# A new hand-out of one order for 1,418 steps on five engines

## The chip, the cores and the metric

The kernel runs on one core of a Trainium2 chip. The metric is device time in microseconds (us). TensorE (PE) multiplies matrices, VectorE (DVE), ScalarE (ACT) and GpSimd (POOL) do elementwise work, SyncE (SP) issues all transfers on one queue. Each engine works through its own list of instructions in order, and waits where an operand or a buffer isn't ready.

## The reference

A linear attention with a decaying state, and behind it a token-mixing and channel-mixing network. B, H, S, D = 4, 8, 768, 48, so the model width is 384; everything is float32.

```python
for t in range(S):                       # per batch and head
    cur = np.einsum('bhd,bhe->bhde', u[None] * kt, vt)
    y[:, :, t] = np.einsum('bhd,bhde->bhe', rt, state + cur)
    state = wt[:, :, :, None] * state + np.einsum('bhd,bhe->bhde', kt, vt)
...
h = xt @ U @ V                           # x: attention's result, mixed over time, rank 32
u = x + h.transpose(0, 2, 1)
ch = np.maximum(u @ w_ch1, 0.0) @ w_ch2  # 384 -> 1536 -> 384
return u + ch
```

## The kernel before, in words

**Staging.** The sequences are cut into chunks of 128 tokens: 24 chunks g, six for each batch. The network works on seven blocks of tokens, 384, 384, 512, 512, 512, 384 and 384 wide. Blocks 0 and 1 hold the first batch, blocks 5 and 6 the last, and blocks 2 to 4 the two between; a block can start as soon as its chunks and the mixing of their batches are done. So attention of later chunks and the network of earlier blocks run side by side, and blocks 5 and 6 wait for the last batch.

**Steps.** The kernel first makes a list of 1,418 named steps (`step`), each a small function with an engine, the steps it comes after, and the buffers it takes and uses. Nothing is issued then. Names carry the chunk, the weight part or the block with its part:

- Transfers (SP): LW, LRK, LKR, LV load decay, r and k, and v of a chunk (L359 to L371); LRAW a part of the weights (L284); LCK loads a part again for the check at the end; OUT sends a result (L919).
- Weights, which are split in a high and a low float32 part: E (L309), C2 (L302), C3 (L315), ADD (L322), HI (L332, L334), SUB (L339).
- Attention of chunk g: the scans F (L390) and Q (L405), each two instructions, with T (L397, L399) and R (L437, L438) between; RP (L413) and KS (L418, L420, a pair) scale r and k; PR (L418, L420) and MD (L496), or RK (L448), RU (L451) and RED (L455), make the diagonal; SEL and SEL2 (L469 on ScalarE, L475 on GpSimd) place it; KT, KN or KD (L522, L531, L679) turn k; AM (L544) gives the scores, CP (L551) masks them; DS (L561), ZA (L593) and ZM (L593 to L602) carry the state; YA and YZ (L622 to L649) give y; XE (L666) copies it out.
- Turning x: XT and XN (L735, L739) or, from chunk 12 on, XD2 and XD1 on VectorE (L716, L714), four steps of four transposes each.
- Mixing for a batch: GA (L761), G4 (L767), SELM (L772), GS (L776), GSL (L781).
- A block's network: HP (L815), UADD (L820), UH (L825, L827), UL (L831); then, for 12 parts f, UP (L864, nine matmuls), HH (L869 on ScalarE, L871 on VectorE) and HL (L875); then, for 3 column parts of 4 steps each, DN (L898, nine matmuls), and O (L916).
- CK and CM (L1083, L1089) look over the weights that LCK has loaded; GUARD (L429) does that for the decay.

**What sets the order.** A string ORDER, L62 to L103, three characters for each step. The first two are the step's number in base 64. The third says how: if it is odd the step runs on its second engine (`alt`, such as VectorE in place of ScalarE for an HH, or GpSimd in place of VectorE for an RP), and half of it is the number of warm-up matmuls on a blank tile that are issued ahead of the step (`lead`). `plan` (L131) reads the string, hands out the buffer slots in that order, first freed first, and returns the list; L1138 to L1140 then issue the steps. An engine's own list is thus the order of its steps in the string, and a transfer's place on SP's queue and its buffer come from it too. Slots: 20 big ones, two each for decay, v, F, turned k and state, one for Q, three PSUM tiles for the matmuls with `f`, `hp`, `ga`, `gb` and the turned tiles in common.

```python
i, how = DIGITS.index(ORDER[n]) * 64 + DIGITS.index(ORDER[n + 1]), DIGITS.index(ORDER[n + 2])
...
if how % 2:
    s.eng = s.alt
s.lead = how // 2
for buf in s.take:
    buf.slot = free[buf.pool].pop(0)
```

Of the kernel before, what the change touches and what calls it, by code (L numbers as in the profile page):

```python
# [59 lines left out]

DIGITS = "0123456789ABCDEFGHIJKLMNOPQRSTUVWXYZabcdefghijklmnopqrstuvwxyz+-"
ORDER = (  # L62
    "2x02y03002z03203M00J03713603303P00K03N03R03n03m03503412-03800L03V03C03903E03W13A13B10M03X03S03113v04B03U03F0"
# [4 lines left out]
    "0z04U10+01D07g14q00Z05504W00o07u00a04t04X01E04s05D00b00s07x00c05C17a03L00p01F04v04w07h04u15E01G03k05008300e0"
    "7c00q08014x04803l04905F07i18K05G00d17z05H04Y04y00r15I00-04Z01H10u04z08U05K05J01I00g05L07b07j15M07m05N00v07k0"
    "7W00f01007+00h00t07n05O07y15P07qC1101205Q07-18o08N00i07l05R00j00w05U05Y05V07r05S01d08A05Z00k07s05W08w05T17o0"  # L70
    "8L01W05a08108801J08901P05X11e07t05b11315o48V15l01f07p18415+08W15p01Q01K01g01L00x01X05m05q08501M00y08611N05-1"
    "5c01h06005d07w05f05n01O11Y01r06108711R08C01Z06201S08B01i08P05g01T01a08F02A09e08X06305e08G06S05h08Q05i08x08D0"
    "1k01b06T01j18T01U08Y11V15x01s02C01m08H08R01c08O05j05r08S08y11n08n05y02B05z05k02308z01t08c02D01u01l01o02E08m0"
    "5s07Y18Z15t06708M01y01v08p08d06801p01q08r08v08E11w02O02F06405u06901x11+02502402H08+11-02605v01z08h06U02008i0"
    "6502G12V09n08u16A02106B06605w08s02709M02I02202808a09h08t08j06C06W02P02J08b06D02Q08q12K02L02916E08-18e02M06X0"
    "2R08f09202X09002N02S09C09309102j08g12l06G06V12c02Y06a02T06H09402W02Z09E09709802k02a08k09F09N18l02U19906I02b1"
    "6b06Y09g09i16Z16F06c08I09A02m09H02e06d16J08J02f02q02d06K06h09I09L09D02g09B06i19j02s09506j09O16t06M02n06n09o0"
    "2o02h12t06u16o06v07602r09K16p02i19f02u09P09J07902p02v06N06O0B709Q19R0B80771Bh07A0BH09G12w09U07B09k09616w06x0"
    "BA06y0780BG0BY06P09S09T09p09q06z09m09V0BF0BX0BC09l16Q09r06k0BD07306+06L09W0Ba06l16m06R0BE19u0BI17409Z09s0BJ0"
    "9a09t19X0750C109v0C206q06-0BB06e0B909Y1C406f0Bc0BK09b0BN0700710BR06r09w0CB06g0C90Bd09x0Be1Bg0BO09c0C516s0CA0"  # L80
    "D70BL0BP0BQ09y0BM1CT0Bb17C0Bi07D0Bf0CC07209z09d07E09+0C60DZ07F0Cd0C709-0Bj0Cz0Bn0BS0BT0BV0A00Ce1Bk0BU1Br0A10"
    "CW0A20A30Bo0Da0Bl0CV07I0Bm0D80BZ07J0CU07K0Bp0CH0CI0CD07G0A40A50C81D60CE0A60Bs0A707L0A90D90AA07O0Bq0DA0Cf0DQ0"
    "C+0AB0AD0CJ0A80AE0Cb0HW07P07Q07R0AF0CF0CG17M0D00Bt07H0AC0Bu0G60CK0AG0Cg0CX1BW0Cj0Db0CL0H00CY0Bw0Bx07S07N0AQ0"
    "AT0HX0CZ0Ca1GW0Cc0Ck0C30D20Ac0AR0DP0AS0AW0AU0GX0CM07T0DB1Cn0Cl0Ch0CN0By0D50CQ0AV0DS0GN0Ad0DC1AX0Dc0F+0Bv1Bz0"
    "CR0Ai0Ae0D10CO0AY0Aj0CP1D30GY0Ci1AZ0D41DD0AN0CS0Aa0Ak0Cm0AO0HY0DE0DU0AP0AH0Co0Al0Cp0Fy0DH0DX0Cs0Ct0DV0G70DF0"
    "Ab0DT1Cq0Am0AI0F-0DW1AK0DI0Cr1DY0An0Cu0AJ0Ao0C-0B+0DM0DG0GM0DN0Dd0AL0Cv0G50Df0DJ0Af0Ap0AM0G10DR0De0Ku0DK0GZ0"
    "Ar0Dg0DO0G20Aq0Ga0Cw0GP0DL1Ag0As0Ah0Gs0Dh0Di0At0Cx0Dj0Dk0Dl0Au0B-0Dm0G80Cy0C00Dn0Ax0Ay0G90H10Av0Fz0Az0G31G40"
    "GR0Lh0GQ1A+0G00A-0Do0Dp0Dq0GG0Dr0Ds0H20GS0Gb1B10GC0Dt0Du0Dv0Dy0H30B20GV0GA1E00GD0Gt0B30GU0Dz0E10Dw0Gv0D+0Gx0"
    "Dx0B40IS0E20E31Lq0GE0HM0GO0Gc0D-0EG0EH0LV0GB1E40Gw0HP0G+1Aw0E50G-0HN0B50IT1E60Ls0IU0Eb0EI0EJ0GF0Li0EV0HU0HQ1"
    "EK0Gd0Ec0Lj0H40HZ0EL0EM0EW0Ed0GI0GH0EN0GK0Kv0GT1Gg0Ew0LS0Ge0HO0I00EO0Kw0GJ1EX0B60Gh0Ex0Hc0ES0Gy0LT0Gz1Gf0ET1"  # L90
    "H51EA0LU0B00E70II0EU0Gi0HR0LX0LW0GL0Lr0Gl0IV0Gm0E80HA0EB0HS0ED0E90Ha1HV0EC0EE0H60Gn0EF0LJ0Hb0Hd0IL0I10EY0Ee0"
    "EP0L70HB0EQ0I21IR0Hs0EZ0Gu0Gj0I30Ht0ER0Gk1Ea0Ef0Eg0Hv0E+0H70E-0F20HT0Eh0Ek0H80Hx0Ey0H+0He0HF0HG0H90LL0Hy0Hg0"
    "F00HC0F30El0Ei0L80Em0En0IJ0I60LK0HH0Eq0I70F40Er0Hu0Hz1HD0Es0K+0F51L40I41Hf0Et0Go0HI0F10IN0Ez1HE1LY0IW1Ln0Hh0"
    "HJ0Gp0FR0IM0L90I50Eo0I80FS0I90FL0Eu0HK0K-0FI0Ej0Hl0Ev0FM1IO0Hm0Hi0HL0IA0FN0Hw1FJ0FT0Hj0Hk1Lt0Gq0Ep0F90IB0LD0"
    "Hn0F60IX0F70IC0Kr0FA1IP1La0IF0IG0IQ0FK0Ho0F80ID0Lv0Lp0IE1L00Hp0LZ0IY0FF0L60FG0FO0FB0FX0Gr0Hq0IZ0FP0IH0IK0Hr0"
    "Ia0FQ0Ib0FY0LA0Ih0Lu0Lo0FH0FC0FZ0Ic0Id0Ie0FD0FE0Fa0If0Ig0Fg0Kt0Ii0Fb0Ij0LF0Ik0Fh0Il0Im0Fc0In0Ir0Io0Is0Jp0Ip0"
    "Iv0Jq0Jt0Iw0M00Ju0Ks0L50FU0Fd0Fe0It0FV1FW0Lw0Fi0Ff0H-0Iq0Fj0Fm0Ix0Fn0Iu1Iy0Jr1Fo0Fk0Fp0Fs0Ft0Fq0JC0JR0M10Fu0"
    "JS1JT0Fv0JD0Lz0Fw0J00JE0Js0JF0Jv1Lx0LB0J10Jx0Le0LC0J20M20Iz0JG0Jy0Ly0J30J40LM0Lg0L-0I+1I-0LE0Lf0J50JU0J90JH0"
    "Lb0JO0JA0L10JV1JB0J60JP0JW0JI0JQ0JL0J70JM0J80JN0JX0JY0JJ0L+0Jz0JK0Fr0JZ0Ja0Jd0Fl0Jb0Je0Kx0Jf0Jg0Jj0Lk0Jk0Ld0"
    "LP0Jw0J+0Jh0LG0Ll0KQ0KR0Lm0KS0Ji0LR0Fx0KB0Jl0L20KC0KT0KU0L30LQ0Jm0KD0KV0KK0KL0LO0Jc0KM0J-0Jn0KH0Lc0LH0KI1KE0"  # L100
    "KJ0K01KF0KG0K80K50K10K20K60K91M30Kz0LN0K70KN0K30K40KO1M50LI0KA0M40Ky0KZ0KW0KX1Ka0KP0Kb0M60KY0M70M80Kc0Kf0Kg0"
# [1123 lines left out]
```

## Time and profile before

| what | value |
|---|---|
| time, median of 3 runs | 435.9 us (435.53 to 438.2) |
| the profiled execution: time, span | 435.73 us, 433.9 us |
| mean granted TensorE clock | 0.969 |
| instructions | 10499 |
| PE, DVE, ACT, POOL busy | 417.4, 344.5, 188.7, 137.7 us |
| moved by transfers | 57.29 MB |

The span goes from the first instruction of the program to the end of the last; the time also holds what lies around it. Busy time counts what overlaps once. Ends of matmuls are modelled, so a short wait between matmuls can be hidden in a busy PE.

### The profile page before, as it was taken

The page shows a single profiled execution, that of the slowest core. Times are in us where ns is not written, and L with a number is a line of the kernel's source. Part 1 is how long each engine was busy: PE and PEld are TensorE (multiplying, and loading weights), DVE is VectorE, ACT ScalarE, POOL GpSimd, SP SyncE. Part 2 cuts the span into 40 slices and gives each one's busy share as a digit, 9 for nine tenths or more (in the row PEclk, how much of TensorE's full clock was granted, in tenths as well). Part 3 has the DMA queues.
Part 4 walks back from the last instruction along what each step waited for, and adds up shares of the span by engine and source line. Part 5 has one row for each costly group of instructions (what it writes and reads, how often), then busy time and mean ns, then how long its engine had stood idle before and what let it go on. Part 6 is the DMA issues. An engine that isn't in the chain of part 4 may idle for free.

```text
span 433.9 us, 10499 instructions
## 1 busy us (share of the span) xinstructions
PE 417.4 (96%) x4150; PEld 361.9 (83%) x4150; DVE 344.5 (79%) x791; ACT 188.7 (43%) x536; POOL 137.7 (32%) x182
## 2 busy tenths in 40 slices
...
GB/s 281 330 283 263 296 168 213 112 191 160 255 147 190 99 269 126 44 49 135 7 155 127 162 95 48 79 184 141 52 22 39 0 133 98 73 105 66 2 39 42
DMA packets 23913, 57.29 MB, mean 132 GB/s; under 512 B 2864, under 2 KB 7856, under 8 KB 23856
## 3 DMA queue, kind: packets, MB, share of 16 engines
...
q8 instruction: 34, 0.56, 0.5%
...
HBM read 51.81 MB, written 4.72 MB: 130 GB/s over the span
## 4 chain that ended last, share of the span: by engine, by line
PE 73%; DVE 18%; ACT 3%; DMA 2%; issue 2%; POOL 0%; DVEq 0%
PE f L898 29%; PE f L864 25%; PE aps L544 4%; DVE kn L679 3%; DVE xn L716 3%; PE y L622 2%; DVE hid L875 2%; DVE xn L714 2%; PE dS L561 2%; PE y L632 2%; DMA v<-in_vS 2%; DVE A L551 1%; PE trd L496 1%; DVE F L390 1%; PE trk L522 1%
## 5 line engine op out<-in xcount | busy, mean ns | idle before, releaser
L864 PE MATMUL f<-u,w1h 128*128 128x384 f32 (+1 forms) x504 | 147.7, 364 | 1.8 <-DVE hid L875 1.1
L898 PE MATMUL f<-hid,w2h 128*128 128x384 f32 (+1 forms) x504 | 148.1, 364 | 0.0
L864 PEld LDWEIGHTS f<-u,w1h 128*128 128x128 f32 x504 | 92.9, 188 | 14.5 <-DVE hid L875 2.9
L898 PEld LDWEIGHTS f<-hid,w2h 128*128 128x128 f32 x504 | 92.9, 188 | 10.1 <-issue 0.7
L869 ACT ACTIVATE hid<-f 128x384 fp32r<-128x384 f32 (+1 forms) x67 | 35.9, 541 | 138.3 <-PE f L864 124.7
L864 PE MATMUL f<-u,w1l 128*128 128x384 f32 (+1 forms) x252 | 90.8, 360 | 0.0
L898 PE MATMUL f<-hid,w2l 128*128 128x384 f32 (+1 forms) x252 | 90.7, 360 | 0.0
L875 DVE SCALAR_TENSOR_TENSOR hid<-f,hid 128x384 fp32r<-128x384 f32 (+1 forms) x84 | 49.8, 608 | 22.0 <-ACT hid L869 21.0
L898 PEld LDWEIGHTS f<-hid,w2l 128*128 128x128 f32 x252 | 47.4, 188 | 4.7
L864 PEld LDWEIGHTS f<-u,w1l 128*128 128x128 f32 x252 | 47.4, 188 | 4.1
L679 DVE STREAM_TRANSPOSE kn<-rk 32x128 f32<-32x128 f32 x160 | 48.3, 302 | 2.4
L469 ACT ACTIVATE A<-ident,dv 128x128 f32<-128x128 f32 x136 | 43.0, 394 | 4.3 <-PE f L898 4.2
L916 DVE TENSOR_TENSOR xT<-f,xT 128x384 f32<-128x384 f32 (+1 forms) x21 | 12.8, 610 | 35.5 <-PE f L898 35.4
L322 POOL TENSOR_TENSOR cva_w<-cva_w,raw_w 128x384 int32<-128x384 int32 x24 | 26.1, 1098 | 45.4 <-ACT raw_w L309 18.6
L831 POOL TENSOR_TENSOR u<-xT,u 128x512 fp32r<-128x512 f32 (+1 forms) x11 | 12.8, 1169 | 85.4 <-ACT u L825 64.3
L413 POOL TENSOR_TENSOR rk<-rk,Q 128x512 f32<-128x512 f32 x18 | 21.6, 1201 | 52.3 <-DVE Q L405 34.9
L405 DVE TENSOR_TENSOR_SCAN Q<-w,starts,qd 128x258 f32<-128x258 f32 x48 | 33.2, 732 | 0.3
L551 DVE COPY_PREDICATED A<-maskf,aps 128x1024 f32<-128x1024 uint32 x24 | 31.5, 1311 | 0.3 <-PE aps L544 0.2
L390 DVE TENSOR_TENSOR_SCAN F<-w,qd 128x259 f32<-128x259 f32 x48 | 30.4, 673 | 1.2 <-DMA w<-in_wT 0.8
L716 DVE STREAM_TRANSPOSE xn<-xT 32x192 f32<-32x192 f32 x80 | 29.6, 370 | 1.1
L544 PE MATMUL aps<-rk 48*64 48x128 f32 (+1 forms) x768 | 24.2, 270 | 0.9 <-POOL rk L413 0.9
L544 PEld LDWEIGHTS aps<-rk 48*64 48x64 f32 x768 | 20.7, 147 | 5.1 <-issue 2.8
...
## 6 DMA issues: line engine op xcount, KB each, us to landing
...
```

What stands on the lines that cost most here:

```text
L322: lambda: nc.gpsimd.tensor_tensor(out=d["to"].bitcast(I32), in0=d["a"].bitcast(I32), in1=d["e"], op=ALU.add),
L390: nc.vector.tensor_tensor_scan(out=back(F), data0=back(st["w"]), data1=back(qd, OVER * h), initial=1.0, op0=ALU.mult, op1=ALU.add)
L405: nc.vector.tensor_tensor_scan(out=st["Q"][:, a:e], data0=st["w"][:, a:e], data1=qd[:, a - OVER * h : e - OVER * h], initial=starts[:, h : ...
L469: nc.scalar.activation(to, one, AF.Copy, scale=dv[:, NP * i + j : NP * i + j + 1])
L544: nc.tensor.matmul(aps[HP * a : HP * a + HP, i, jj, s0:P], rk[r, 1, jj, k0 : k0 + HP], rk[r, 0, jj, s0:P], start=True, stop=True,)
L551: nc.vector.copy_predicated(to, mask2, new)
L679: nc.vector.transpose(to[32 * j : 32 * j + 32, :, 32 * i : 32 * i + 32], src[32 * i : 32 * i + 32, :, 32 * j : 32 * j + 32])
L716: nc.vector.transpose(to[q, :, :, r], src[r, :, :, q])
L864: nc.tensor.matmul(ps, wt[:, f, ct, :], u[ct][:, z], start=(m == 0), stop=(m == 8))
L869: nc.scalar.activation(h[:, 0], d["ps", f], AF.Relu)
L875: nc.vector.scalar_tensor_tensor(out=h[:, 1], in0=d["ps", f], scalar=0.0, in1=h[:, 0].bitcast(F32), op0=ALU.max, op1=ALU.subtract)
L898: nc.tensor.matmul(d["o", ct], wt[:, 4 * ct + part, f - 3 * part, :], hid[f][:, z], start=(part == 0 and m == 0), stop=(part == 3 and m == 8),
```

## The change

Only the string ORDER is another one; the steps, their code and the slots are the same. The diff replaces all lines of the string; the first two and the last of each show the form:

```diff
 ORDER = (
-    "2x02y03002z03203M00J03713603303P00K03N03R03n03m03503412-03800L03V03C03903E03W13A13B10M03X03S03113v04B03U03F0"
-    "3p03w03Y03T11404A00N03r03D03Z13b03O00003Q13G00Q03a10O03d03s03H14D03e04b04K03I04F04E14I13u13c02+01601503t1010"
...
-    "Kh0Kd0Ke0Ki0Kl0M90Km0Jo0Kn0Kj0Kk0Ko0Kp0Kq0"
+    "2x02y02z03000J03M03203N03603713800K03103302-00L03503C03m03413P03903A10M03E03V03n04B03W13B10N03U00O03R03X03S0"
+    "3p03F00003r03Y03D03Z13b03T13G04A03Q11403w03d03s03x04K04D03a14J00Q03O03e03v00R00S04a03u13H10T04E10200P01604I1"
...
+    "Kg0Kh0M80Ki0Kl0M90Km0Kn0Ji0Kj0Kk0Ko0Kp0Kq0"
 )
```

Read with `plan`, the two strings compare like this.

- 85 steps have another engine. Between ScalarE and VectorE: 14 HH come to VectorE and 13 leave it, 5 T each way, 2 UH come and 1 leaves, 1 HI and 2 ZM come. Between GpSimd and VectorE: 4 KS, 3 RP, 2 SUB, 2 UL, 1 RK and 1 RU come to VectorE; 4 SUB, 4 UL, 3 RK, 3 RU, 1 KS and 1 RP leave it. Between ScalarE and GpSimd: 8 SEL and SEL2 go to GpSimd, 5 to ScalarE. VectorE has 490 steps for 488, ScalarE 312 for 320, GpSimd 130 for 124.
- Warm-up matmuls: before 6 ahead of YA 6 and 2 ahead of UP 0.4; after 1 ahead of MD 5, 3 ahead of HP 0.0 and 3 ahead of UP 0.8.
- VectorE up to UL 0.2, the last step that the first UP needs: 82 steps before, 84 after. F 8 stands behind it now; T 0, RK 8 and RP 7 stand ahead.
- VectorE up to the last of the four XD2 3.5. Gone: HH 1.2, 1.5, 1.10, 3.8, 4.1; KS 20; RK 12, 15, 23; RP 21; RU 9, 10, 22; SUB w19, w20, w22, w24; T 8, 12, 18, 20, 23; UL 1.0, 4.0, 4.2. New: HH 0.6, 1.11, 4.3, 4.6; KS 8, 11, 19, 22; RK 22; RP 7, 11, 15; RU 23; SUB w111, w210; T 0, 11, 13, 17, 21; HI w28; ZM 18, 19; CK 7, 8.
- VectorE around HL 1.6. Before: RP 10, HH 1.10, HL 1.11, Q 11, F 12, HL 1.6, HL 1.10, CP 10. After: Q 11, HH 1.11, F 12, RED 10, HL 1.11, RP 11, F 13, R 12, O 0.2, Q 12, CP 10, HL 1.6.
- TensorE around the same place. Before: UP 1.3, UP 1.10, UP 1.11, DN 0.2.1, DN 0.2.2, AM 10, UP 1.6, DN 0.2.3, KT 10, UP 1.7. After: UP 1.5, DN 0.2.1, UP 1.11, AM 10, KT 10, DN 0.2.2, UP 1.7, DN 0.2.3, UP 1.9, UP 1.6.
- TensorE around DS 3. Before: MD 5, DS 3, AM 4, KT 4, XT 0.0, YA 3. After: KT 4, AM 4, XT 0.2, YA 3, DS 3.
- SP's queue ahead of LV 3. Before, among others, LKR 7, LKR 6 and LRK 6; after LKR 6, LKR 8, LRK 7 and, new, LRAW w18.
- TensorE from YA 23 to DN 4.1.3: the same 22 steps in the same order, and the same steps ahead of them. In block 6, UP 6.8, DN 6.0.0, UP 6.11, DN 6.0.1 before; UP 6.8, UP 6.3, DN 6.0.0, DN 6.0.1 after.
- SP: LRK 23 was issued after LRK 22, in a slot that YZ 20 and KD 20 leave; now it stands behind OUT 3.1, LCK 22, LCK 15 and LCK 7, in a slot that DN 3.2.3 leaves.

## Rows read from the trace of the kernel before

**Rows 1.** The busy table of the page: us, share of the span, instructions.

```profile
PE 417.4 (96%) x4150; PEld 361.9 (83%) x4150; DVE 344.5 (79%) x791; ACT 188.7 (43%) x536; POOL 137.7 (32%) x182
```

**Rows 2.** Windows: stretch, length, busy PE, PEld, DVE, ACT, POOL, granted clock, DMA share, GB/s.

```profile
0.00:59.00 59.00, 52.01 (x895) 42.41 (x896) 56.62 (x124) 50.54 (x154) 34.91 (x46) 0.80 0.83 284
59.00:321.40 262.40, 259.79 (x2690) 221.15 (x2688) 249.96 (x587) 118.73 (x330) 97.79 (x131) 1.00 0.41 130
321.40:328.00 6.60, 5.26 (x25) 3.11 (x25) 3.35 (x7) 2.02 (x5) 0.99 (x1) 1.00 0.00 1
328.00:428.40 100.40, 100.32 (x543) 95.26 (x543) 34.04 (x74) 17.38 (x48) 4.04 (x5) 1.00 0.20 62
```

**Rows 3.** Timeline of TensorE, 310 to 330: start, us, line, shapes, idle before.

```profile
321.43 0.53 PE L761 MATMUL ga<-xn,U_sb 128*32 128x192 f32 x8 [0.75 <-DVE xn L716]
322.57 0.89 PE L772 MATMUL gb<-g,sel 128*96 128x384 f32 x2 [0.61 <-ACT g L767]
...
326.37 0.91 PE L815 MATMUL hp<-Vst,gs 96*128 96x384 f32 x2 [0.47 <-DVE xT L820]
```

**Rows 4.** Waits of VectorE, 58.8 to 321.4: us in total, times, longest.

```profile
DVE hid L875 <- ACT hid L869: 2.3, 5, 1.1
DVE hid L871 <- PE f L898: 1.4, 1, 1.4
DVE Z L593 <- PE dS L561: 0.7, 1, 0.7
```

**Rows 5.** Groups of VectorE by shape: count, busy us, mean ns, idle before.

```profile
L413 DVE TENSOR_TENSOR rk<-rk,Q 128x512 f32<-128x512 f32 x6 | 4.4, 740 | 0.0
L339 DVE TENSOR_TENSOR w1l<-cva_w,w1h 128x384 fp32r<-128x384 f32 x7 | 3.9, 559 | 0.0
...
L420 DVE TENSOR_TENSOR rk<-rk,F 128x256 f32<-128x256 f32 x7 | 2.9, 416 | 0.0
L418 DVE TENSOR_TENSOR rk<-rk,F 128x256 f32<-128x256 f32 x7 | 2.9, 412 | 0.0
...
L831 DVE TENSOR_TENSOR u<-xT,u 128x512 fp32r<-128x512 f32 x3 | 2.0, 677 | 0.0
```

**Rows 6.** Timeline of VectorE, 104 to 121.

```profile
109.94 1.06 DVE L413 TENSOR_TENSOR rk<-rk,Q 128x512 f32<-128x512 f32 x1
112.35 0.56 DVE L871 TENSOR_SCALAR hid<-f 128x384 fp32r<-128x384 f32 x1 [1.35 <-PE f L898]
113.22 0.56 DVE L875 SCALAR_TENSOR_TENSOR hid<-f,hid 128x384 fp32r<-128x384 f32 x1 [0.31 <-ACT hid L869]
113.69 1.38 DVE L405 TENSOR_TENSOR_SCAN Q<-w,starts,qd 128x258 f32<-128x258 f32 x2
114.99 1.25 DVE L390 TENSOR_TENSOR_SCAN F<-w,qd 128x259 f32<-128x259 f32 x2
117.37 1.02 DVE L875 SCALAR_TENSOR_TENSOR hid<-f,hid 128x384 fp32r<-128x384 f32 x2 [1.13 <-ACT hid L869]
118.31 1.33 DVE L551 COPY_PREDICATED A<-maskf,aps 128x1024 f32<-128x1024 uint32 x1
```

**Rows 7.** Waits of VectorE, 4 to 58.8.

```profile
DVE F L390 <- DMA w<-in_wT: 0.8, 2, 0.5
```

**Rows 8.** Timeline of TensorE, 30 to 45.

```profile
35.27 0.31 PE L561 MATMUL dS<-v,kn 128*48 128x48 f32 x1 [1.79 <-DMA v<-in_vS]
```

**Rows 9.** Timeline of GpSimd, 104 to 121.

```profile
110.40 1.48 POOL L339 TENSOR_TENSOR w2l<-cva_w,w2h 128x384 fp32r<-128x384 f32 x1
...
112.70 1.02 POOL L339 TENSOR_TENSOR w2l<-cva_w,w2h 128x384 fp32r<-128x384 f32 x1
```

**Rows 10.** The chain that ended last: start, us, what.

```profile
258.89 2.06 PE f L864 x9
...
392.11 1.56 PE f L864 x9
```

More of the change, by code (lines that the diff above doesn't have):

```diff
@@ L62 @@
 ORDER = (
-    "2x02y03002z03203M00J03713603303P00K03N03R03n03m03503412-03800L03V03C03903E03W13A13B10M03X03S03113v04B03U03F0"
-    "3p03w03Y03T11404A00N03r03D03Z13b03O00003Q13G00Q03a10O03d03s03H14D03e04b04K03I04F04E14I13u13c02+01601503t1010"
-    "3x00S00R00P00204L01703f00T04a00C04103J03y03-04J03z10308203+14M04P04-00D00U04N14G04d03o04004Q00404H13q14f04j0"
-    "3g14+03h00504207e04k00V04e10l04g05103i00601807U00W14O14l04i13j05700707f10E00801904h10m00F05814R00G04307X0441"
-    "4m00907V00H04505304605214C04n15904o11B04S05405A10A07Z00I01A14T05B14r00X04p00n00Y07v01C05600B13K04707d04V04c0"
@@ L68 @@
[L68 to L101, printed above, removed]
-    "Kh0Kd0Ke0Ki0Kl0M90Km0Jo0Kn0Kj0Kk0Ko0Kp0Kq0"
+    "2x02y02z03000J03M03203N03603713800K03103302-00L03503C03m03413P03903A10M03E03V03n04B03W13B10N03U00O03R03X03S0"
@@ new lines @@
+    "3p03F00003r03Y03D03Z13b03T13G04A03Q11403w03d03s03x04K04D03a14J00Q03O03e03v00R00S04a03u13H10T04E10200P01604I1"
+    "4F01503I03t12+01700303y04b03o04L04G00l07e04+03c03-01803z14d03q10503J04j00100U04M04104f03+14-00V00C03f04204N1"
+    "4H14k03h04g00405101B00W10704O14e14h14i14007v00603g13i07f17U04l01900800m05708U04m04R04n15814C03j00E01A10F00D0"
+    "0G03K04P04o18200H00n04S05300907X05924504305407Z07d03L01C05A14604Q03k04p00X00o00A00I07g14704r01D05214803l00B1"
+    "5500Z01E04410Y04V04T05604q04c07V07u04W05B11F00z00a05C10b00s04U10c00p07a07c04s07x04X05005D04t00e07h00+08K04v0"
@@ new lines @@
+    "0q05E04w01G00d17b04u10u04Y00r14x00v04Z01H11d07i15F00g00-08015G04908V14y05H04z07m01008300h05I07j15K08n05J05L0"
+    "1100f07W01W05M00t07z07n07k05N07+00i07l05O01201I07q00w07y15P01e00j05Q67-01P07r05R05U05V00k05S05Y05Z05T15W05a0"
+    "5X18A05b11317o01J08807s00x01K08418L07t05+61L05o01M00y08901f05-15l08N07p16001N01g08W17w01r08101h08501O05p05m0"
+    "8w05c08615n05q01Q08718P01y01Y01X05f01R06101S01Z08B08C05g01T08M08T01a01i08F08Q05d06205h01k05e08x01b08G06308X0"
+    "1U05x08R01l08S16S02A05r06T01V11c11m08O11s08Y11j01t01u05i05y01n05s05z08c08m08D08Z11o01v08y05j05u08E12B08o05t0"
@@ new lines @@
+    "5k08d06708H01w02C02309e05v18h08z01x01z08i02D01p01+02E06406805w09D08a06908p07Y16A01q02502406B06502H01-02602c0"
+    "2006C08r08+16608s02F08b02106W09h02708q18u18t02O02j02G12202I09006D08-12802909106X09208v02Q02J08e08j09C09i02e0"
+    "6a06G06U06H02K02L02R09308f06E09F09702V06b06V02M02P08g19809408I02S02k08k06Y02T02d02f02N06c02U19L06Z12l08J06d1"
+    "9G12X02W06I02Y02Z09509E09H02g09909M02q09f09I02a1B708l02m06J09A02b19B06h09j02n06K09N16n02o02h16o06M06p06t02s0"
+    "2i12r02p16i16N09J09616F06u09m16j07909K12t06v09U09n0BH09k02u09O09o07A12v02w0BA0B809P09S06O09Q0BX09T07B09p06L0"
@@ new lines @@
+    "9R1D706z06P07309l0Ba0BF09q0BC0740BI06Q0BD06w06x06+09V0BG06R09W0BJ0D80C10BB16y09r0BK09s09u09Z0BN09a09t19b06k0"
+    "750Bc0BY0BL0BE16l09g0Bh09X06m0760Bd0770Bg07806-09v07006e06f0BO09Y1Bi06q0Cd06r06g0D90BM0BR09w09x0710BP0Bf09c0"
+    "9y06s0720C40B907C0GW09d0Bj0C20Be1BZ0DA07D0Bn0Bk09z0BS07E0C60Ce0C709-0C90BV09+0A00CU0A10CB0BQ0CA0BT0CC0Br0GX0"
+    "Bo0Bb07F0CT0Bp0Cz0CD0Bl1CW0LS0A207I07G0A30CY07J0Bq0A40C81C51Cf07K0A50CH0A60D00Bm0BW0A907L0AA07O0DB0CE07M0BU1"
+    "CF1AD0CI0Bs07P0A70CZ07Q0D20AE0DZ07H0D60AB07R0C+0CJ0AF0Cc0CG17S0Bt0DC1CX1Bw0Bx0A80Da0Ca0CK0AC0Cg0C30HW0D30Bu0"
```

18 lines of the change are left out of this document (added).

## The prediction, made before the changed kernel was run

> **What bounds the kernel now.** I read four views in this order: the busy table with the chain's shares, the windows by stage, the waits of each engine, and the timelines at the places where a wait decides. All sums start from the profiled execution, 435.73 us, of which 433.9 are the span and 1.8 lie around it; the median of the three runs shown is 435.9, so the profiled one is ordinary.
>
> The busy table has two engines near their limit: TensorE 96% of the span, VectorE 79% [rows 1]. VectorE's share is an average over two different halves, so the stages have to be looked at one by one [rows 2]. Up to 59.0 us, where the first UP starts, VectorE is busy 56.62 of 59.0 and the granted TensorE clock is at 0.80 of full, a mean over its two levels: this stage ends when VectorE has got through its queue. From 59.0 to 321.4 TensorE is busy 259.79 of 262.4 and VectorE 249.96: both are full at once. From 321.4 to 328.0 TensorE has 5.26 of 6.6. From 328.0 to 428.4 it has 100.32 of 100.4 and VectorE only a third. The 5.5 us behind that are one addition, one transfer and the end. The clock is at 1.00 from 59.0 us on.
>
> Why cut at 321.4? There the last transposes of the attention (the four XD2 3.5) leave VectorE, and TensorE, which has run out of other work, takes them up: GA 3.1 starts after 0.75 us of idling for VectorE's `xn`; the mixing matmul `gb` then waits 0.61 for ScalarE, and the `hp` matmuls 0.47 for VectorE [rows 3]. After them come blocks 5 and 6, with work in plenty. So the time is, to a good approximation: the moment when VectorE has finished with the attention (321.4), plus some 6.6 us of a chain that hardly overlaps, plus 100.4 of TensorE alone, plus the tail. A microsecond that VectorE loses anywhere before 321.4 is paid at the end, unless another wait of VectorE swallows it. These waits are few: the three largest groups between 58.8 and 321.4 sum to 4.4 us [rows 4].
>
> **The change part by part.** Every step stays; 85 of the 1,418 have another engine, the order differs, and there are 7 warm-up matmuls for 8. TensorE's own work is thus the same but for one warm-up, and these stand where it waits for something else: nothing.
>
> *Start, to the first UP.* VectorE's steps up to UL 0.2, which the first UP needs, are the same but for F 8, which goes behind, and T 0, RK 8 and RP 7, which come in front of it. F is two instructions whose place in the order alone changes; T is tiny; RK is a step of 0.55 and RP one of 0.73 [rows 5]. A later F takes 1.25 [rows 6], so it is 1.25 out against 1.28 and a T in: nothing. VectorE's whole wait for transfers in this stage is 0.8 us [rows 7], so making transfers more tolerant can give back at most 0.8, and lose if a load now comes late. TensorE does show one late load here: a DS waits 1.79 us for `v` at 35.27 [rows 8]. In the new order that step stands behind AM 4, KT 4 and YA 3, and the wait will be gone. I give it no gain, because VectorE, not TensorE, sets the pace in this stage and did not stop for it. The new order also asks for one load of weights more ahead of this `v` (w18; LKR 8 and LRK 7 stand for LKR 7 and LRK 6), which the later place of DS 3 covers. Value 0, between -0.8 and +1.8, the size of the one wait that the stage shows.
>
> *Middle: VectorE's load before 321.4.* Of the steps that stand ahead of the last XD2 3.5, these leave VectorE: 5 HH, 1 KS, 3 RK, 1 RP, 3 RU, 4 SUB, 5 T, 3 UL. These come: 4 HH, 4 KS, 1 RK, 3 RP, 1 RU, 2 SUB, 5 T, 1 HI, 2 ZM, 2 CK. Net: the T cancel, of the HH one 384-wide leaves. I price all that is 384 wide by the row of SUB, 3.9 us for 7, 0.55 each: HH -1, RK -2, RU -2, SUB -2, UL -1, against HI +1, ZM +2, CK +2 makes -3 steps, -1.65. (ZM has no row on VectorE in this trace; the row of SUB is the nearest of its size, and nothing from 0.3 to 0.7 would move the sum by more than 0.5.) KS is a pair of 2.9/7 = 0.41 each, +3 pairs, +2.5. RP is 4.4/6 = 0.73, +2, +1.5. UL 512 wide is 2.0/3 = 0.67, -2, -1.3. Sum +1.0 us [rows 5]. It is on the path in full, since nothing behind 321.4 can take it up. ScalarE loses 8 steps and POOL gains 6; both are idle for more than half of this stage, and cost nothing by themselves.
>
> One thing could change the price of a step on VectorE. At 109.94 an RP there took 1.06, where the group's mean is 0.74, and the POOL step beside it, a SUB from 110.40, took 1.48 where the next one took 1.02 [rows 5, 6, 9]. The Trainium skill has a rule for it ("SBUF — State Buffer", section "SBUF: two separate sides"): a VectorE instruction with two SBUF inputs and a POOL instruction that reads SBUF exclude each other for a whole instruction. The row agrees in direction and size. By the rule alone, moving RP and KS to VectorE while POOL gets more to do is a poor trade; its result is the second rival.
>
> *Middle: VectorE's waits.* The largest cluster lies at 112 to 118 us, where VectorE had caught up with TensorE: HH 1.10 waits 1.35 us, HL 1.11 0.31 and HL 1.6 1.13 [rows 6]. In the new order RP 11, F 13, R 12, O 0.2, Q 12 and CP 10 stand directly ahead of HL 1.6, none of which needs UP 1.6: RP 0.73, F 1.25, Q 1.38 and CP 1.33 alone are 4.7 [rows 5, 6]. On TensorE UP 1.6 comes later too, behind UP 1.7, DN 0.2.3 and UP 1.9 but ahead of UP 1.10, two steps of 1.56 or 3.1 in all [rows 10]. The 1.6 that is left over covers the wait of 1.13, so I take it as gone: -1.1. HH 1.10 has gone to ScalarE, but HH 1.1 and HH 1.11 stand in its neighbourhood and can wait in the same way, so its 1.35 I leave in. All other waits I take as replaced by as many. Bounds of this term: -2.8 (the whole cluster gone) and +4.4 (the three groups doubled).
>
> *Chain at 321.4 and the end.* From YA 23 to DN 4.1.3 TensorE's order is the same step by step, so the chain of GA 3.1, SELM, GS, GSL, HP and UADD stays at its 6.6 us. In block 5 VectorE gets seven HH and gives two away, at 0.55 each, with an HL of the same size behind: 1.1 per UP, while the nine 384-wide matmuls of an UP take 1.56 us [rows 10]. It keeps up. One late place: UP 6.3 is now the last UP and DN 6.0.1 needs its HL one DN later, 1.56 us for HH and HL in a row, 1.1; up to 0.5 us could show. The load LRK 23 is issued later: its buffer is freed by DN 3.2.3. Six UPs of block 4, 2.06 each [rows 10], stand between that and AM 23, so there are over 12 us for a transfer and two POOL steps. Value 0, to +0.5.
>
> Sum: 435.73 + 0 + 1.0 - 1.1 + 0 = 435.6 us. No change that can be measured. A measurement of this kernel can tell about 1%, 4.4 us, from no change.
>
> **The rivals.**
> *VectorE's queue meets its partners too early (slower).* Each HH and HL is queued in order behind and before scans, transposes and CP steps. With 14 HH put on VectorE and 13 taken off, and TensorE's UPs in another sequence, the meetings move. Where an HH waits, all behind it wait: the scans F and Q of the next chunk, then POOL's RP, AM, CP. Price: 0.3 to 1.35 a meeting [rows 6], paid in full at 321.4. It decides from some 5 us more of waits than now, eight or so new ones of 0.6: with 5.5 it is 435.6 + 5.5 = 441.1. For it: neither TensorE nor VectorE has slack there [rows 2]. Against it: only 6% of the steps have another engine and the sequences are close.
> *The lock (no change, on the slow side).* Three RP and four KS are new on VectorE. If each met a POOL step and took 0.4 longer, as the one of 1.06 did against 0.67 to 0.74, that is 2.8: 438.4. Against it: 7 two-input steps of the other kinds leave.
> *The plan closes the gaps (faster).* TensorE's idle time is 2.6 us between 59.0 and 321.4 and 1.3 to 328.0 [rows 2]. If VectorE came in early enough to close all of it: 435.73 - 3.9 = 431.8; the modelled ends of matmuls hide perhaps as much as another microsecond, so 431. Nothing else can be saved behind 59.0, as the work is the same. Against it: VectorE has 1.0 more to do, not less.
> *The change does not do what it says.* In this trace only 1.79 us of TensorE and 0.8 of VectorE hang on transfers [rows 7, 8]; an order that bears halts better has then nothing to bear, and the time stays at 435.7.
>
> **How the numbers follow.** Forecast 0.50, no effect at all 0.14, the lock 0.10: all three within 1%, 0.74. Slower by over 1%: 0.18, the first rival. Faster by over 1%: 0.08, and that only with the hidden microsecond, since 431.8 is itself within 1%. The range reaches down to 432.0, near the closed gaps, and up to 441.0, the first rival's price; about 0.08 is left out below and 0.10 above.
>
> **What would show it.** In the changed profile: the first UP at 58 to 60.5 us; no wait of DS for `v` at 35; VectorE's busy time to the last XD2 3.5 at some 1 us more than now and the three largest groups of its waits at 3 to 5 in sum; GA 3.1 at 320 to 323; from there to the end 112 us as now. The forecast is wrong if GA 3.1 comes after 326 (then VectorE's list of waits names the place), or if the stretch behind it is longer than 114 us, which would put the cause in blocks 5 and 6.

## The result, and the profile after

| kernel | median | lowest to highest, runs | ratio to before, 95% interval |
|---|---|---|---|
| before | 436.28 us | 435.53 to 438.2, 6 | 1 |
| changed | 441.31 us | 440.5 to 442.85, 6 | 1.0115, 1.0094 to 1.0136 |

The changed kernel is slower by 1.15%, some 5.0 us; the forecast was no change. The profiled execution took 441.53 us, its span is 439.8 us.

The busy table of the changed kernel, which answers to [rows 1]:

```profile
PE 418.1 (95%) x4149; PEld 361.5 (82%) x4149; DVE 348.3 (79%) x796; ACT 182.9 (42%) x513; POOL 143.0 (33%) x191
```

The windows of the changed kernel, with the columns of [rows 2]. The cuts lie within 0.2 us of the same events: the first UP of the list (UP 0.8 here, UP 0.4 before), GA 3.1, UP 4.8 and O 6.2.

```profile
0.00:63.40 63.40, 52.48 (x894) 41.69 (x895) 57.92 (x125) 51.30 (x154) 33.17 (x45) 0.81 0.84 286
63.40:327.20 263.80, 260.03 (x2690) 221.45 (x2689) 251.44 (x590) 115.18 (x317) 105.77 (x142) 1.00 0.41 128
327.20:333.80 6.60, 5.21 (x25) 3.07 (x25) 3.67 (x9) 1.50 (x4) 0.00 (x0) 1.00 0.21 60
333.80:434.30 100.50, 100.39 (x543) 95.31 (x543) 34.71 (x75) 14.89 (x40) 4.08 (x4) 1.00 0.14 46
```

Against [rows 2] the first stretch is 63.4 us long for 59.0, the second 263.8 for 262.4, the other two are equal within 0.1. So in these two executions the start lost 4.4 us, the middle 1.4, and blocks 5 and 6 nothing. In the start VectorE is busy 1.3 us longer and idle 5.5 us for 2.4; in the middle it is busy 251.4 for 250.0 and idle as long as before (12.4).

Where does TensorE stand in the start? Its timeline in the changed kernel, to be held against [rows 8]:

```profile
33.38 0.48 PE L196 MATMUL trd<-blank 128*128 128x384 bf16 x1 [2.90 <-ACT dv L501]
...
46.06 0.90 PE L544 MATMUL aps<-rk 48*64 48x128 f32 x32 [1.30 <-POOL cva_w L322]
...
53.57 0.30 PE L645 MATMUL y<-rk,Z 128*32 128x128 f32 x1 [1.65 <-issue]
```

The first is the warm-up of MD 5, which now stands ahead of YA 2, DS 2, YZ 2 and AM 4 and waits for the PSUM tile that DV 4 on ScalarE has to leave. The second is AM 5. Its row names GpSimd, but GpSimd's results had been there: CP 4 on VectorE, which has to leave the one tile of scores, ended at 45.96. The third is the last of sixteen matmuls of YZ 5, which waits for no step at all. In the kernel before, AM 5 does not wait:

```profile
43.30 0.90 PE L544 MATMUL aps<-rk 48*64 48x128 f32 x32
```

DV 4 is itself held up. Some steps ahead of it ScalarE stands at E V0 for the load of V0; the first row is the changed kernel's, the second e2's, which has the same steps up to there:

```profile
30.26 0.56 ACT L309 ACTIVATE raw_V<-raw_V 96x384 int32<-96x384 uint32 x1 [1.03 <-DMA raw_V<-in_V]
32.73 0.56 ACT L309 ACTIVATE raw_V<-raw_V 96x384 int32<-96x384 uint32 x1 [4.19 <-DMA raw_V<-in_V]
```

In the kernel before, that wait is 0.13 us. So a part of the start's waiting is a load that comes late, handed on from ScalarE to TensorE. And VectorE:

```profile
5.84 0.65 DVE L399 COPY tots<-F 128x4 f32<-128x4 f32 x1
...
9.93 1.23 DVE L420 TENSOR_TENSOR kr<-rk 128x256 f32<-128x256 f32 x1
...
43.38 1.39 DVE L405 TENSOR_TENSOR_SCAN Q<-w,starts,qd 128x258 f32<-128x258 f32 x2
44.68 1.27 DVE L551 COPY_PREDICATED A<-maskf,aps 128x1024 f32<-128x1024 uint32 x1
...
56.29 1.33 DVE L551 COPY_PREDICATED A<-maskf,aps 128x1024 f32<-128x1024 uint32 x1 [2.02 <-ACT A L469]
...
59.24 0.55 DVE L781 TENSOR_TENSOR gs<-gb,gs 32x384 fp32r<-32x384 f32 x1 [0.35 <-ACT gs L776]
```

The same places of VectorE in the kernel before:

```profile
9.35 0.42 DVE L420 TENSOR_TENSOR kr<-rk 128x256 f32<-128x256 f32 x1
...
41.25 1.32 DVE L551 COPY_PREDICATED A<-maskf,aps 128x1024 f32<-128x1024 uint32 x1
...
43.65 1.37 DVE L405 TENSOR_TENSOR_SCAN Q<-w,starts,qd 128x258 f32<-128x258 f32 x2
...
52.89 1.31 DVE L551 COPY_PREDICATED A<-maskf,aps 128x1024 f32<-128x1024 uint32 x1
...
54.23 0.56 DVE L781 TENSOR_TENSOR gs<-gb,gs 32x384 fp32r<-32x384 f32 x1
```

Read both from the end. Before, VectorE goes from CP 4 (41.25) through CP 6 (52.89) to GSL 0 (54.23) without a wait. Changed, CP 4 starts at 44.68, with Q 6 ahead of it instead of behind, and then the path leaves VectorE: AM 5 at 46.06, YA 4, XE 4, YA 5, YZ 5 with its 1.65, XT, GA 0, SELM 0, GS 0. VectorE gets to CP 6 and waits 2.02 us for ScalarE, and GSL 0 comes 5.0 us later than before. From AM 5 to GSL 0 it is 13.2 us for 10.9.

The middle: TensorE's timeline of the changed kernel, with four waits that the kernel before does not have at these steps (GA 2.1, UP 3.3, AM 23, GA 3.0), and GA 3.1, which answers to [rows 3].

```profile
221.54 0.53 PE L761 MATMUL ga<-xn,U_sb 128*32 128x192 f32 x8 [0.81 <-DVE xn L716]
...
257.88 0.50 PE L864 MATMUL f<-u,w1h 128*128 128x512 f32 x1 [0.44 <-DVE hid L875]
...
309.35 0.90 PE L544 MATMUL aps<-rk 48*64 48x128 f32 x32 [0.51 <-issue]
...
319.31 0.85 PE L761 MATMUL ga<-xn,U_sb 128*32 128x384 f32 x8 [0.85 <-DVE hid L875]
...
327.27 0.53 PE L761 MATMUL ga<-xn,U_sb 128*32 128x192 f32 x8 [0.69 <-DVE xn L716]
```

The first four sum to 2.6 us. VectorE's three largest waits in the middle, which answer to [rows 4], sum to 5.6 for 4.4:

```profile
DVE xT L820 <- PE hp L815: 2.3, 3, 0.9
DVE hid L875 <- ACT hid L869: 2.1, 3, 1.0
DVE w2l L339 <- ACT w2h L332: 1.2, 1, 1.2
```

### The profile page after: what moved, and what is told of

It reads as the page before. It is cut to its first block, busy times and chain, and to the rows that moved or that the text cites. A ratio compares the mean times of both kernels' runs of the same rounds, so it can differ in the third digit from the quotient of the medians.

```text
span 439.8 us, 10477 instructions
## 1 busy us (share of the span) xinstructions
PE 418.1 (95%) x4149; PEld 361.5 (82%) x4149; DVE 348.3 (79%) x796; ACT 182.9 (42%) x513; POOL 143.0 (33%) x191
## 4 chain that ended last, share of the span: by engine, by line
PE 58%; DVE 29%; DMA 5%; issue 3%; SPq 1%; ACT 0%; POOL 0%; DVEq 0%; POOLq 0%
PE f L898 29%; PE f L864 19%; DVE xn L716 5%; DVE hid L875 4%; DVE kn L679 4%; PE aps L544 2%; DVE Q L405 2%; DVE A L551 2%; DMA w<-in_wT 2%; DVE F L390 2%; DMA rk<-in_rkT 1%; DVE cva_w L315 1%; PE y L622 1%; DMA raw_w<-in_w 1%; DVE xn L714 1%
## 5 line engine op out<-in xcount | busy, mean ns | idle before, releaser
L869 ACT ACTIVATE hid<-f 128x512 fp32r<-128x512 f32 (+1 forms) x66 | 35.2, 542 | 128.0 <-PE f L864 116.6
L469 ACT ACTIVATE A<-ident,dv 128x128 f32<-128x128 f32 x124 | 39.3, 395 | 10.1 <-PE f L898 8.7
L831 POOL TENSOR_TENSOR u<-xT,u 128x512 fp32r<-128x512 f32 (+1 forms) x13 | 15.4, 1190 | 74.2 <-DVE u L827 30.3
L413 POOL TENSOR_TENSOR rk<-rk,Q 128x512 f32<-128x512 f32 x16 | 19.1, 1195 | 61.3 <-DVE Q L405 37.5
```

The costliest lines, as they stand in the source:

```text
L469: nc.scalar.activation(to, one, AF.Copy, scale=dv[:, NP * i + j : NP * i + j + 1])
L869: nc.scalar.activation(h[:, 0], d["ps", f], AF.Relu)
```

## The experiments

Each is another string ORDER; the diffs show the engines' lists that come of it. Where two orders are joined, each step keeps the engine of the order that it is taken from. "Loss" is the ratio less 1, times 436 us.

| run | median, us | before beside it | ratio, 95% interval | loss, us |
|---|---|---|---|---|
| e1 | 442.01 | 436.06 | 1.0127 (1.0103 to 1.0151) | 5.5 |
| e2 | 440.94 | 436.06 | 1.0089 (1.0054 to 1.0125) | 3.9 |
| e3 | 440.17 | 436.06 | 1.0093 (1.0065 to 1.0121) | 4.1 |
| e4 | 443.74 | 436.06 | 1.0164 (1.0145 to 1.0184) | 7.2 |
| e5 | 441.92 | 435.76 | 1.0123 (1.0087 to 1.0159) | 5.4 |
| e6 | 440.99 | 435.76 | 1.0118 (1.0068 to 1.0168) | 5.1 |
| e7 | 445.36 | 435.76 | 1.0199 (1.0163 to 1.0234) | 8.7 |
| e8 | 452.91 | 435.76 | 1.0389 (1.0341 to 1.0437) | 17.0 |
| e9 | 440.62 | 436.45 | 1.0092 (1.0064 to 1.0119) | 4.0 |
| e10 | 441.49 | 436.45 | 1.0120 (1.0093 to 1.0148) | 5.2 |
| e11 | 440.65 | 436.45 | 1.0099 (1.0071 to 1.0127) | 4.3 |
| e12 | 439.99 | 436.45 | 1.0096 (1.0067 to 1.0124) | 4.2 |
| e13 | 439.08 | 436.21 | 1.0061 (1.0041 to 1.0080) | 2.7 |
| e15 | 438.84 | 436.21 | 1.0060 (1.0037 to 1.0083) | 2.6 |
| e16 | 439.05 | 436.60 | 1.0065 (1.0041 to 1.0088) | 2.8 |
| e17 | 441.19 | 436.60 | 1.0110 (1.0081 to 1.0140) | 4.8 |
| e18 | 441.95 | 436.60 | 1.0124 (1.0099 to 1.0149) | 5.4 |
| e19 | 437.48 | 435.84 | 1.0037 (1.0025 to 1.0049) | 1.6 |

**Where is the loss? e1, e2, e11, e13, e15: one order up to a cut, the other behind it.**

```diff
 e1: ORDER of the changed kernel
-its steps up to UP 0.0
+the steps up to UP 0.0 in the order of before (325 steps)
 e11: the same, cut behind CP 7 (342 steps); e13: as e11, without HH 0.9, HH 0.0, LV 9
 e2, e15: the reverse of e1 and e13
```

> The steps up to UP 0.0 stand as in the kernel before, all later ones as in the changed kernel. Theory 'start' (some 4.6 us of the loss lie ahead of the first UP, 1.2 us between there and GA 3.1, nothing behind): first UP at 58.5 to 59.5 us, time 437.5, between 436.8 and 438.3. Rival 'middle' (VectorE's meetings between 59 and 321 us are the cause, and a late first UP would be made up for): the time stays near 441.

> The reverse: the steps up to UP 0.0 as in the changed kernel, all later ones as in the kernel before. Theory 'start': first UP at about 63 us, GA 3.1 at about 326, time 440.5 (439.8 to 441.2). Rival 'middle': 436 to 437, since the old order of the middle would take up the late start.

> As e1, the start as in the kernel before and the rest as changed, but cut 17 places later in the string, behind CP 7, where the two orders have done the same steps but for three. If e1's 442.0 came from its cut (there TensorE stood 1.48 us at UP 0.6 and 0.54 at YA 7, in places where neither whole kernel stands), this kernel takes 437 to 438. If the changed order of the middle costs it, whatever the start: 441 to 442 again, with GA 3.1 at 326 or later from a first UP at 59 to 60.

> The start as in the kernel before, the rest as changed, cut behind CP 7 so that each order has done the same steps but for LRK 9, LRAW w23 and R 8: HH 0.9, HH 0.0 and LV 9 stand where the changed order has them. In e1 and e11 LV 9 stood in the start's part and took the buffer of LV 8, LV 8 held SP until YA 7, and w21 came late (ScalarE waited 3.2 us for it in e11), which no whole kernel does. Theory 'start' (some 4 us lost ahead of the first UP, 1 to 1.5 behind it): first UP at 58.5 to 59.5, GA 3.1 at 322.5 to 323.5, time 437.0 to 438.0. Rival 'the middle costs it too' (with an early start the changed middle loses 2.5 us or more, so the two losses don't add up): 439 or more, GA 3.1 at 324 or later.

> The reverse with the same cut: the start as changed, the rest as in the kernel before. Theory 'start': first UP at 62.5 to 64, the stretch from there to GA 3.1 as long as in the kernel before (262.9 us), time 440 to 441. Rival: the old middle takes up part of it, 437 to 439.

e1 lost as much as the whole change, though its first UP came at 60.6, and e2 about as much. That would make each half guilty of all of it. But e1 and e11 had a seam: LV 9, issued with the start, took a buffer that LV 8 then waited for, w21 behind LV 8 came late, and TensorE stood 1.48 (e1) and 1.00 us (e11) at UP 0.6. The clean pair, nine executions each, is the better measure: the changed rest alone loses 2.7 us, the changed start alone 2.6, together 5.3, and the whole change 5.0. Each interval excludes no loss as well as the whole loss, so both halves lose. Neither run took the time that theory 'start' expected (437 to 438 for e13, 440 to 441 for e15); both came out as the rivals said, though the old middle did not take up anything in e15. The windows of e13 (up to the first UP, from there to GA 3.1):

```profile
0.00:60.60 60.60, 53.44 (x896) 43.15 (x897) 56.44 (x124) 50.22 (x154) 34.85 (x46) 0.89 0.84 290
60.60:324.70 264.10, 259.99 (x2689) 221.31 (x2688) 251.83 (x590) 115.21 (x317) 103.75 (x141) 1.00 0.41 130
```

and of e15:

```profile
0.00:63.00 63.00, 53.19 (x894) 42.62 (x895) 58.68 (x125) 51.15 (x154) 33.12 (x45) 0.95 0.81 273
63.00:325.20 262.20, 259.97 (x2690) 221.18 (x2688) 250.72 (x588) 118.69 (x330) 99.52 (x132) 1.00 0.40 128
```

The middle is 264.1 long with the changed order and 262.2 with the old one, 262.4 in the kernel before. The other traces agree. Counted from the warm-up ahead of the first UP to GA 3.1, the four kernels with the old middle have 262.65 to 263.33 us, and nine with the changed one 264.37 to 264.94 (those with a seam, with moves in the middle, and e8 are left out). So by the traces the middle costs some 1.5 us, less than e13's 2.7.

The start is not as steady. Counted to the same warm-up, it was 58.5 in the kernel before, and 58.5 to 60.6 in the five joined kernels that have its order there; with the changed order 62.9 in the changed kernel, and 62.5 (e15), 64.9 (e18) and 65.0 (e2). The two groups don't meet. In e13, at 60.1, F 6 waited 1.84 us for LW 6, which landed at 34.11 for 31.73 though it had been issued no later. So some of e13's 2.7 may belong to its start, and the loss of the start lies between the 2.6 of e15's median and the 4.4 of one execution of each kernel. The granted clock does not explain the loss: in the start it was 0.81 for 0.80, and 0.89 and 0.95 in e13 and e15, which lose all the same.

**What in the start? Single engines' lists: e5 to e8.**

```diff
 e5, ScalarE:
-GUARD 3 | GUARD 2
+GUARD 2 | GUARD 3
 e6, SP of the changed kernel up to LV 7: order of before;  e7, SP of before: order of the changed kernel
 e8, TensorE up to UP 0.0 and ScalarE up to XN 1.0 of the changed kernel: order of before
```

> The changed kernel with GUARD 2 ahead of GUARD 3 on ScalarE, nothing else. There GUARD 3 waits 0.98 us for its transfer at 16.6, GUARD 2 ends at 18.3 behind it, and SP stands with LW 4 and all transfers behind it until 18.3 (16.2 in the kernel before). Theory 'transfers' (SP is held at buffers, the pipe moves 6.15 MB up to 24 us for 7.40, some 3 us too few, and the chain of the start runs through late loads): LW 4 is issued by 17.0, the later loads 1.3 us earlier, first UP at 61.6 for 62.9, time 440.0. Theories 'queues' and 'VectorE's own work': under 0.3 us, 441.

> The changed kernel, but SP's own list up to LV 7 stands in the order of the kernel before; the other four engines keep the changed order. Theory 'transfers': LRK 4 and LRK 5 land some 4 us earlier, LV 4 is not held to 38.7, first UP at 60, time 438.5. Theory 'queues' (the lists of TensorE and ScalarE lose it): first UP still at 62 to 63, time 440.5 to 441.5.

> The kernel before, but SP's own list up to LV 7 stands in the order of the changed kernel. Theory 'transfers': first UP 1.5 to 3 us later than 58.5, time 438 to 439. Theory 'queues': 436 to 437.

> The changed kernel, but TensorE's list up to UP 0.0 and ScalarE's up to XN 1.0 stand in the order of the kernel before (the engine of each step stays as changed, and so do VectorE's, GpSimd's and SP's lists). Theory 'queues': the waits of 2.9 and 1.3 us of TensorE ahead of MD 5 and AM 5 go, first UP at 59.5 to 60.5, time 438.5. Theory 'transfers': the old lists meet the late loads and wait there instead, first UP at 62 to 64, time 441 to 442.

In e5 LW 4 was issued at 17.0 for 18.3, as meant, and nothing came of it (5.4 us). With e6 (5.1) the theory "transfers" falls in the form that it was put in: LRK 4 and LRK 5 landed 3.3 and 5.0 us earlier, and CP 4 on VectorE started at 44.68 all the same, to the hundredth. But V0 landed no earlier (30.14 for 30.15), so the wait at E V0 stayed; no run removed it alone. e7 fits neither theory: 8.7 us, three times the highest that was expected. There ScalarE, in its old order, stands at E w10 until w10 lands at 34.16, and ZM 1, which DS 2 needs, is queued behind it. TensorE's timeline of e7:

```profile
38.68 0.41 PE L560 MATMUL dS<-Z,ident 128*48 128x48 f32 x4 [6.39 <-ACT Z L602]
```

e8 lost 17.0. An engine's list is tied to the others' so closely that taking one back alone says little about what it costs in its own company.

**Single steps of the start: e3, e4, e9, e10, e12.**

```diff
 e3, TensorE:                          ScalarE:
-KT 3 | MD 5 (1) | YA 2 | DS 2 | YZ 2  -E V0 | ... | DV 4 | SEL 4 | XE 1
+KT 3 | YA 2 | DS 2 | YZ 2 | MD 5      +XE 1 | E V0 | ... | DV 4 | SEL 4
 e4: T 0 from VectorE to ScalarE behind SEL2 0; RK 8 behind SUB w17
 e9, VectorE:
-Q 6 | CP 4
+CP 4 | Q 6
 e10: e9, and DS 2 ahead of MD 5, ZM 1 ahead of E V0, LV 2 behind LRK 5, LRK 7 behind LRAW w13
 e12: e3 and e9
```

> The changed kernel with MD 5 behind YZ 2 on TensorE, without its warm-up, and with XE 1 ahead of E V0 on ScalarE, both as in the kernel before. Theory 'queues' (TensorE stood 2.9 us at MD 5 and was then held by XE 1, and that late TensorE is what CP 6 waits 2.0 us for at 56 us): AM 4 at 37 to 38 instead of 40.7, CP 6's wait gone, GSL 0 some 2 us earlier, time 439.2. Rival 'VectorE's own work' (VectorE was busy without a stop from 38 to 54 us, so what delays GSL 0 is its own list): AM 4 comes earlier but GSL 0 by under 0.5, time 441. Rival 'code' (the 1.65 us in which TensorE waits for no step within YZ 5 at 51.9 to 53.6, beside the instruction transfer of 16 KB at 51.2): that wait stays, and with it 1.5 us or more of CP 6's; time 440.5 to 441.3.

> The changed kernel with T 0 back on ScalarE behind SEL2 0, and RK 8 behind SUB w17 on VectorE. Theory 'VectorE's own work': these two cost VectorE 0.66 and 0.55 ahead of GSL 0, so GSL 0 comes 1.2 us earlier, time 440.1. Theory 'queues' and rival 'code': CP 6 waits for TensorE and ScalarE in any case, its wait grows from 2.0 to about 2.6 by RK 8's 0.55, and only T 0's share at the very start can show (0 to 0.6 us): 440.7 to 441.3.

> The changed kernel with CP 4 ahead of Q 6 on VectorE, two neighbours changed round, nothing else. New theory 'late handing over' (the list of VectorE reaches CP 4 at 44.68 for 41.25, of which Q 6 is 1.30; AM 5 needs the PSUM tile that CP 4 leaves, so TensorE stands 1.30 us at 46.06, and from there to GSL 0 the chain runs through TensorE and ScalarE, not VectorE): AM 5 at 44.8, GSL 0 1.3 us earlier, time 440.0. Rival 'VectorE's own work' (its steps ahead of GSL 0 are the same in number, so their order among each other can't matter): AM 5 earlier, GSL 0 not, time 441.3.

> The changed kernel with five steps moved within the start: CP 4 ahead of Q 6, DS 2 ahead of MD 5, ZM 1 ahead of E V0, LV 2 behind LRK 5, LRK 7 behind LRAW w13. Theory 'late handing over': each takes some tenths out of the places where one engine stands for another or for LW 6's late landing; first UP at 60.8 to 61.5 for 62.9, time 439.3 to 440. Rival 'VectorE's own work': 441.

> The edits of e3 and e9 together. Theory 'late handing over': e3 alone gave 440.2, so with CP 4's 1.0 to 1.3 the time is 439.0, no wait of TensorE for its own instructions in YZ 5, first UP at 60. Rival 'VectorE's own work': 440 to 441, as e3.

e9, AM 5 on TensorE:

```profile
45.15 0.90 PE L544 MATMUL aps<-rk 48*64 48x128 f32 x32 [0.67 <-POOL cva_w L322]
```

It came 0.9 us earlier, GSL 0 2.1, and the first UP 1.4; the loss is 1.0 us less than the changed kernel's, e3's 0.9 and e12's 0.8, with intervals that overlap the changed kernel's, and without adding up. e10 had its first UP at 61.0, as expected, but in the fastest of its four executions, and its median did not move. In that execution ScalarE did not wait at E V0. In e3 AM 4 stayed 3.4 us late: MD 5 no longer stood in front, but XT 0.1 then waited 2.18 us for ScalarE and KT 4 1.06 us for DV 5, which VectorE has behind F 6. The 37 to 38 that "queues" expected was wrong. e4 is against "VectorE's own work": with T 0 and RK 8 gone from ahead of GSL 0, the time rose by 2.2 us, further than any theory had it. Why is not shown; in its profile the loads of LW 5 and V0 held VectorE for 2.08 and ScalarE for 2.89 us.

**What in the middle? e16 to e19: VectorE's steps that TensorE stood behind.**

```diff
 e19, VectorE, on e13:
-XD2 2.5 | RED 20 | XD2 2.5 | XD2 2.1 | R 19 | XD2 2.5
+XD2 2.5 | XD2 2.5 | XD2 2.1 | XD2 2.5 | RED 20 | R 19
-RED 23 | HL 3.2
+HL 3.2 | RED 23
 e16: e19, and CP 22 ahead of ZA 21, HL 4.6 ahead of HH 4.3
 e17, e18: these four moves on e12 and on the changed kernel
```

> e13 (start as before, rest as changed) with four meetings of the middle put right on VectorE: RED 20 and R 19 behind the last XD2 2.5, HL 3.2 ahead of RED 23, CP 22 ahead of ZA 21, HL 4.6 ahead of HH 4.3. Theory 'meetings' (in the changed middle TensorE stands 0.81 us at GA 2.1, 0.44 at UP 3.3, 0.51 at AM 23 and 0.85 at GA 3.0, each behind one step of VectorE that nothing near needs; these are its 1.6 us): the four waits are under 0.4 in sum, time 437.1 to 437.6, 1.5 to 2 less than e13's 439.1. Rival 'VectorE's load' (the prediction's: GA 3.1 comes when VectorE has got through its list, whatever the order): the waits go and GA 3.1 waits longer in their place, time 439.

> e12 (the changed kernel with three edits of the start) with the same four moves in the middle. Theory 'meetings': 438.2 to 438.6, from e12's 440.0. Rival 'VectorE's load': 440.

> The changed kernel with the four moves of the middle alone. Theory 'meetings': 439.3 to 439.8, from 441.3. Rival 'VectorE's load': 441.

> e16 with two of its four moves only: RED 20 and R 19 behind the last XD2 2.5, and HL 3.2 ahead of RED 23; CP 22 and HL 4.6 stand as in e13, since there e16 lost 1.03 us at DS 22 and 1.00 at UP 4.9, two waits that e13 doesn't have. Theory 'meetings': the 0.87 and 0.46 us that TensorE stood in e13 at GA 2.1 and UP 3.3 stay saved, first UP to GA 3.1 is 263.4 us for e13's 264.7, time 437.8. Rival 'VectorE's load': TensorE is earlier up to AM 22, as in e16, and stands that much longer between there and GA 3.1; first UP to GA 3.1 stays at 264.5 or more, time 439.

e16 stayed at e13's time, and TensorE's timeline says why: two of the four moves made waits of their own, since DS 22 needs the ZA 21 that CP 22 had passed, and UP 4.9 waits for an HL that came later.

```profile
304.85 0.56 PE L561 MATMUL dS<-v,kn 128*48 128x48 f32 x16 [1.03 <-DVE Z L593]
...
311.18 0.50 PE L864 MATMUL f<-u,w1h 128*128 128x512 f32 x1 [1.00 <-DVE hid L875]
```

e17 and e18, with the same four, gained nothing either. With the other two moves alone, e19 took 437.48: a loss of 1.6 us for e13's 2.7. In its timeline TensorE no longer waits at GA 2.1 (sixteen matmuls in one row; e13 stood 0.87 us between its two eights) nor at UP 3.3:

```profile
216.67 1.37 PE L761 MATMUL ga<-xn,U_sb 128*32 128x384 f32 x16
```

From the first UP to GA 3.1 e19's profile has 264.2 us for e13's 264.7, a gain of 0.5 against 1.3 expected, and no more than 0.2 against the changed kernel's 264.4; the intervals of the two medians overlap. By UP 3.3 e19 had gained 0.9 on e13, by AM 23 only 0.5 were left, which is in part what the rival "VectorE's load" expected. So it is shown that the two waits went, and not that they were what the middle costs.

No run points to a kernel faster than the one before.

## Why the prediction was wrong

**The step that failed** is "Start, to the first UP": "Value 0, between -0.8 and +1.8". Measured: 2.6 us by e15's median, 4.4 in the profiled execution. With the middle's two terms below, this made the time 5 us longer; either loss alone would have left it within the range that was given. Its premise, that VectorE sets the pace there, was right for the kernel before: every step of VectorE back from GSL 0 to CP 4 begins as the one ahead of it ends. But the working counted VectorE's steps as a set and found the two sets equal. The sets are indeed nearly equal: ahead of CP 4 the changed list has only T 0 and Q 6 more. By the traces, what counts is when those steps come that hand work to the other engines. CP 4 is 3.4 us later (1.30 of it Q 6, 0.57 T 0, 0.81 the longer PR 1, the rest small waits and steps), and from AM 5 to GSL 0 TensorE and ScalarE need 13.2 us for 10.9, with 1.65 of standing, while VectorE runs dry. The bounds came from the waits that the trace of before had (1.79 and 0.8), and an order that is planned anew makes waits in places that had none: 2.90, 1.30 and 1.65. They allowed for a late load by the size of that one wait; V0 came late, by 1.03 us at E V0 here and by up to 4.19 in another execution. That the wait of DS 3 for `v` would go was right; whether it gave anything can't be told.

What exactly the start's 2.6 us consist of stays open. e3, e9 and e12 took away one or two of TensorE's waits and each gained about 1 us, less than the intervals separate; exchanging whole lists gained nothing; and the wait at E V0 was not tried by itself.

**VectorE's load ahead of 321.4, +1.0**: right in kind and short in size. Between the first UP and GA 3.1 VectorE is busy 251.44 us for 249.96, +1.5 [rows 2]; with the start, which the term's list took in, it is +2.8. The pairs KS and the RP kept their price: 418 ns for 416 and 706 for 740 [rows 5].

**VectorE's waits, -1.1**: wrong, the other step that failed. HH 1.10's and HL 1.6's cluster is not among the largest any more, but others stand in its place: the largest three sum to 5.6 for 4.4, and its whole idle time in the middle is the same. The sum of the two terms was -0.1, measured were +1.4 in the windows and 2.7 by e13. VectorE's 1.5 us of more work with the same idle time make up the 1.4 of the windows, so the prediction's own account, load and no gain in waits, is enough for them; the four waits of TensorE are the same loss seen from its side, and the runs do not tell which of the two sets it.

**Chain at 321.4 and the end**: right. From GA 3.1 to the end of the span 112.6 us for 112.5; the sign that was named, GA 3.1 after 326, came (327.27), and the cause lies ahead of it. That VectorE's list of waits would then name the place was wrong for the middle, where its idle time did not grow.

**The rivals.** "VectorE's queue meets its partners too early" gave 441.1, and the time was 441.3; that is luck, since its place was not where it said: HH and HL wait no longer than before in the middle, and half of the loss or more is ahead of the first UP. What may be true of it is the kind, one step of VectorE put ahead of a step that TensorE waits for; e19 took away two such waits, and its middle hardly shortened. "The lock" shows at two steps that it did not name: T 0 took 0.65 us beside GpSimd's KS 0, where this copy took 0.16 in the mean of the kernel before, and the second half of PR 1 took 1.23 us for 0.42 beside GpSimd's ADD w11, which ran from 9.81 to 10.88. This is no chance: PR 1's half took 1.23 or 1.24 in all thirteen kernels with VectorE's changed start, and 0.41 or 0.42 in the seven with the old one. The RP and KS that came to VectorE met nothing. That the lock costs the start time is argued from these rows; only e4 took one of the two away, with RK 8 moved too, and lost. "The plan closes the gaps" did not come: TensorE idled 3.8 us in the middle for 2.6. "The change does not do what it says": six executions of the changed kernel spread over 2.35 us, six of before over 2.67, and e2 over 4.1 us; nothing here shows that the new order bears a late transfer better, and its start stood 1.0 to 4.2 us at E V0 in the four traces that have it, where the old one, in six, stood at most 0.7.
